# Holding attention's loads back to about 1.2 MB on their way, and issuing each input in two halves

## The chip, the cores and the metric

The kernel runs on one core of one Trainium2 chip. The metric is device microseconds of one execution, and the time given for a kernel is the median of several. One more execution is taken with the hardware profiler; all rows below come from that one. MB are 10^6 bytes, KB are 1024 bytes.

## The reference

All inputs are fp32. A retention (linear attention with a decay instead of a softmax) of 4 batches, 8 heads, 576 positions and 64 channels per head feeds two feed-forward layers over 2304 tokens, with a width of 512 and an inner width of 2048:

```python
scores = (1 / sqrt(64)) * q @ k.T
ret = scores * Dmat            # Dmat[i, j] = gamma_h ** (i - j) for i >= j, else 0
x = (ret @ v) of all heads, as [2304, 512]
h = x @ w_in;  g = max(h, 0) + alpha * min(h, 0);  x = g @ w_out      # "moe"
h = x @ w_in2; g = h / (1 + exp(-1.702 * h));      out = g @ w_out2   # "moe2"
```

## The kernel before

The order on every engine is written out by hand. Work that is not a step's own is put into a list of events by `at(time, ...)`, and `run_to(time)` carries out those that are due, so an event's time is a place in the order and no microsecond.

**Attention** goes over 16 pairs of heads, `PAIRS`, one after the other; I call the work of one pair a step, 0 to 15. In step i, TensorE computes the scores of pair i (`a_scores`, tile `sc`, four chunks of 128 positions), the outer products of keys and values (`a_outer`, tile `st`), then for the pair before it the products within chunks (`a_within`, tile `av`) and across chunks (`a_across`). All its matmuls go through one helper, `mm`, at L353. VectorE multiplies the scores by the decay (`a_evac`, L386) and sums the states; ScalarE scales keys and states (L317).

**Attention's loads** are `a_load(i)`: the 1728 columns of q, k and v of a pair go into a tile `ld` (L309), and its 512 columns of keys in another layout into a tile `kts` (L311). A column is 128 partitions of 4 bytes, so a pair has 0.885 MB and 0.262 MB. Loads 0 to 2 go out before step 0; the first is cut into three transfers, the next two into two. Loads 3 and 4 follow at the end of step 0, and load i+4 at the end of step i. There are five buffers for `ld`, so load i+4 waits for the step that last read its buffer, which is step i+1 at its beginning, as the rows of SP show.

**The queue of SP** issues all of these. Between them, by events, it issues the first weights of layer 1, `w_piece` (L129): rows 0 to 5 of `w1`, two pieces of 1024 columns (0.524 MB) each, into a tile `raw`. Six of the twelve pieces are issued before load 15. Behind load 15 stand the other six, the stores of the first output weights (`plain_store`, L212 and L213), the stores of `evict` (L249, L250), and then the stores of attention's output (`a_store`, L479). Later weights are issued by GpSimd's queue. SP issues in order: a transfer that waits holds up all behind it. The framework counts the landings of SP's transfers in eight counters in turn, so each transfer also waits, before it is issued, for the one eight places ahead of it to have landed.

**From a row of weights to its use**: ScalarE runs `w_sat`, `w_range` and `w_top` (L133, L137, L141) over a landed row, VectorE `w_low` (L148), and both split it into a high and a low part. ScalarE and VectorE too work in order.

**Layer 1** begins when attention ends, with products `h` (L515) and `acc` (L556); layer 1's last part and layer 2 go through `product` (L697) on sums of blocks.

Of the kernel before, what the change touches and what calls it, by code (L numbers as in the profile page):

```python
# [17 lines left out]
DM, DFF = 512, 2048  # L18
# [8 lines left out]
SYNC = mybir.DependencyInfo(mybir.DependencyClass.Sync, mybir.DependencyReason.DATA)  # L27
# [12 lines left out]
NG = 5  # L40
SUM = {1: 0, 2: 1, 4: 2, 5: 3}
RING = ("w6", "X1", "w15", "X2", "X4")
HOME = (0, 7, 2, 3, 4, 5, 6, 15)


@with_exitstack
def kernel(
# [11 lines left out]
    nc = tc.nc  # L59
# [36 lines left out]
    def slot(tag, shape, dtype=F32, name="t"):  # L96
        if tag[0] == "X":
            n = int(tag[1]) - 1
            return xp[n // 2].tile(shape, dtype, tag=f"x{n % 2}", name=name)
        return (wp if tag[0] == "w" else cvp).tile(shape, dtype, tag=tag, name=name)  # L100
# [21 lines left out]
    raws, cvs, wi, wo, x_t, fs, hs = {}, {}, {}, {}, {}, {}, {}  # L122

    def w_load(key, src, home):
        raws[key] = slot(home, [128, 2 * DM, 2], I32, "raw")

    def w_piece(key, src, c, eng):
        f = src[key[1]].rearrange("p (f t) -> p f t", t=2)
        eng.dma_start(out=raws[key][:, c * DM:c * DM + DM], in_=f[:, c * DM:c * DM + DM])  # L129

    def w_sat(key):
        f = raws[key][:, :, 1].bitcast(F32)
# [23 lines left out]
    def w_tile(m, n):  # L156
# [6 lines left out]
        if j not in wi:  # L163
            wi[j] = wp.tile([128, 2, 2, DM], F32R, tag=f"w{HOME[j]}", name="wi")
        return wi[j][:, a], f[:, 0:DM]
# [86 lines left out]
    def bring_wi(j):  # L252
        wi[j] = wp.tile([128, 2, 2, DM], F32R, tag=f"w{HOME[j]}", name="wi")
        nc.gpsimd.dma_start(out=wi[j].bitcast(F32), in_=kept[j // 2][0])
# [8 lines left out]
    def row(key, src, home, load, when, eng):  # L263
        at(load[0], w_load, key, src, home)
        for c, t in enumerate(load):
            at(t, w_piece, key, src, c, eng)
        for t, fn in zip(when, (w_sat, w_range, w_top, w_low)):
            at(t, fn, key)
# [27 lines left out]
    def tmp(what, i, shape):  # L296
        tags = TMP[what]
        return wp.tile(shape, F32, tag=f"w{tags[i % len(tags)]}", name=what)

    halves = (slice(0, 64), slice(64, 128))  # L300
    def kts(i):
        return kts_t[i // 4 % 2][:, i % 4]

    def a_load(i):
        b, p = PAIRS[i]
        t = tmp("ld", i, [128, 1728])
        cuts = {0: (0, 512, 1152, 1728), 1: (0, 1152, 1728), 2: (0, 1152, 1728)}.get(i, (0, 1728))
        for n, (c0, c1) in enumerate(zip(cuts, cuts[1:])):
            nc.sync.dma_start(out=t[:, c0:c1], in_=qkv[b, p, :, c0:c1])  # L309
            if n == (i == 0):  # L310
                nc.sync.dma_start(out=kts(i), in_=kn[b, p])  # L311
        q = [t[:, j:j + 128] for j in (0, 384, 512, 640)] + [t[:, 768:832]]
        k = [t[:, j:j + 128] for j in (128, 256, 832, 960)] + [t[:, 1088:1152]]
        ld[i] = q, k, t[:, 1152:1728].rearrange("p (n d) -> p n d", n=9), t[:, 384:832]
# [272 lines left out]
    def gblk(s, j):  # L587
        if j not in g2:
            n = f"w{HOME[j - 2]}" if j > 1 else ("raw0", "X3")[j]
            g2[j] = slot(n, [128, NG, RN], name="g2")  # L590
# [73 lines left out]
    def r_split(n, q, lo):  # L664
        if n not in ws:
            ws[n] = slot(RING[n % 4], [128, 2, 4, 256], F32R, "ws")
        c = slice(2 * q, min(2 * q + 2, 4 - n % 2))
# [6 lines left out]
    def s_load(r, n):  # L674
        i, h = divmod(n, 2)
        if r:
            home = RING[n % 5]
        elif n in (3, 4):
            home = ("w13", "w8")[n - 3]
            xt2.pop(8 - n)  # L680
        else:
            home = RING[(n - 2 * (n > 4)) % 3]
        t = ws["s", n] = slot(home, [128, 4, 2, 256], F32R, "ws2")
# [243 lines left out]
    with tc.manual_schedule():  # L927
        kts_t = [wp.tile([128, 4, 512], F32, tag=f"w{n}", name="kts") for n in (9, 15)]
        for t, a in ((fades_sb, fades), (vtab_sb, vtab)):
# [5 lines left out]
            out=mask_sb, in_=mask_sb, pattern=[[1, 128]], compare_op=ALU.is_ge, fill=0.0, base=0,  # L935
# [10 lines left out]
        for i in range(3):  # L946
            a_load(i)
# [4 lines left out]
        for i in range(n_a + 1):  # L952
# [34 lines left out]
            for n in (3, 4) if i == 0 else (i + 4,):  # L987
                if n < n_a:
                    a_load(n)
# [4 lines left out]
            out=rise_sb, in0=alpha_sb, scalar1=-1.0, scalar2=1.0, op0=ALU.mult, op1=ALU.add  # L994
# [47 lines left out]
        for r in range(R):  # L1042
            z = r * 2 * NU
            for j in range(NJ):
                u = z + 7 * j
                for t, what in (
# [3 lines left out]
                    if r == 0 and j in (5, 6) and what in ("g22", "g12"):  # L1050
                        t = 8.01
# [114 lines left out]
```

## Time and profile before

| | |
|---|---|
| median of 3 runs | 809.49 us (806.51, 809.49, 809.51) |
| profiled execution, its own time | 809.11 us |
| its span in the profile | 807.4 us |
| PE busy | 795.0 us (98%) |
| DVE, ACT busy | 642.6 us, 528.9 us |
| attention | from the start to about 73.8 us, where the first `h` begins |

The execution's own time is 1.7 us longer than the span, in which the first and the last instruction lie. PE is TensorE's matmuls and PEld its weight loads; both come from one stream of instructions. "issue" in the chain of waits is time in which the engine waited for nothing that the profile shows. The profile lists DMA queues by number: q1 carries the transfers that SP issues, q8 and q14 are of the kind "instruction". A row of DMA issues gives the size of one transfer and the median time from its issue to its landing.

### The profile page before, as it was taken

To read this page: it belongs to the slowest core of one execution; us is meant where nothing else is said; L and a number is where in the kernel's file an instruction comes from. 1 tells how busy PE (TensorE), PEld (TensorE's weight loads), DVE (VectorE), ACT (ScalarE), POOL (GpSimd) and SP (SyncE) were. 2 spreads that over 40 slices of the span, in tenths; PEclk is the share of its full clock that TensorE was granted. 3 is DMA by queue.
4 is the path that set the end of the run, shared out by engine and by line. 5 is a ranking of instruction groups with operands and counts; after the bars stand their busy time and mean duration, and the time that the engine had idled before them with its cause. 6 is when DMAs were issued, how large, how long until landed. Compare 5 with 4: busy or idle time off the path is not lost.

```text
span 807.4 us, 14644 instructions
## 1 busy us (share of the span) xinstructions
PE 795.0 (98%) x5260; PEld 739.9 (92%) x5260; DVE 642.6 (80%) x1195; ACT 528.9 (66%) x959; POOL 83.8 (10%) x104
## 2 busy tenths in 40 slices
PE   9898999999999999999999999999999999999998
PEld 7787888888887888899999999999999999999998
DVE  7776997888485586879999898799777899787775
ACT  6687969887455657456678667667566666566552
POOL 2321122100011111634300000000000000000000
PEclk9999999999999999999999999999999999999999
DMA  9996999865779987597889656996544986446881
GB/s 351 400 347 267 347 325 342 320 240 216 266 248 374 369 279 233 192 335 262 313 345 351 222 166 202 343 313 234 161 136 148 354 289 214 141 131 216 277 276 63
DMA packets 87791, 214.11 MB, mean 265 GB/s; under 512 B 7971, under 2 KB 43811, under 8 KB 79014
## 3 DMA queue, kind: packets, MB, share of 16 engines
q1 hardware_dynamic: 80784, 187.99, 65.5%
q0 software_dynamic: 6784, 25.17, 9.1%
q8 instruction: 41, 0.67, 0.3%
q14 instruction: 32, 0.26, 0.1%
q10 hardware_dynamic: 150, 0.02, 0.0%
HBM read 152.59 MB, written 60.56 MB: 264 GB/s over the span
## 4 chain that ended last, share of the span: by engine, by line
PE 89%; DMA 4%; DVE 3%; issue 1%; SPq 1%; ACT 1%; DVEq 0%; POOLq 0%; ACTq 0%
PE acc L697 32%; PE h L697 25%; PE acc L556 13%; PE h L515 13%; PE av L353 4%; PE sc L353 2%; PE st L353 2%; DMA raw<-in_w_dram 1%; DMA rg<-raw 1%; DMA ws<-sp 1%; DMA ld<-in_qkv_dram 1%; SPq L498 1%; DVE raw L198 1%; DMA x<-part 0%; DVE g L523 0%
## 5 line engine op out<-in xcount | busy, mean ns | idle before, releaser
L108 DVE TENSOR_TENSOR gsf<-g,gsf 128x384 fp32r<-128x384 f32 (+1 forms) x272 | 156.4, 586 | 52.8 <-ACT gsf L103 51.6
L103 ACT ACTIVATE gsf<-g 128x384 fp32r<-128x384 f32 (+1 forms) x272 | 146.0, 542 | 74.7 <-PE acc L697 32.5
L556 PE MATMUL acc<-gsf,wo 128*128 128x512 f32 x576 | 138.3, 389 | 1.1 <-ACT gsf L103 1.1
L515 PE MATMUL h<-x,wi 128*128 128x512 f32 x576 | 138.1, 389 | 0.0
L697 PE MATMUL acc<-gsf,ws 128*128 128x384 f32 x768 | 135.2, 334 | 0.0
L697 PEld LDWEIGHTS acc<-gsf,ws 128*128 128x128 f32 x768 | 133.3, 188 | 0.2 <-ACT x L103 0.2
L556 PEld LDWEIGHTS acc<-gsf,wo 128*128 128x128 f32 x576 | 107.9, 188 | 24.4 <-ACT gsf L103 1.5
L515 PEld LDWEIGHTS h<-x,wi 128*128 128x128 f32 x576 | 108.1, 188 | 22.4
L697 PE MATMUL acc<-x,ws 128*128 128x384 f32 x660 | 128.3, 334 | 0.0
L697 PEld LDWEIGHTS acc<-x,ws 128*128 128x128 f32 x660 | 115.6, 188 | 0.3 <-ACT tm L103 0.3
L697 PE MATMUL h<-x,ws 128*128 128x384 f32 x540 | 107.7, 334 | 0.0
L697 PE MATMUL h<-gsf,ws 128*128 128x384 f32 x576 | 102.0, 334 | 0.1
L697 PEld LDWEIGHTS h<-gsf,ws 128*128 128x128 f32 x576 | 100.0, 188 | 0.4 <-ACT x L103 0.4
L697 PEld LDWEIGHTS h<-x,ws 128*128 128x128 f32 x540 | 94.8, 188 | 0.0
L178 DVE TENSOR_TENSOR tm<-h,tm 128x384 f32<-128x384 f32 x97 | 53.6, 553 | 26.9 <-PE h L697 21.5
L178 DVE TENSOR_TENSOR g<-g 128x384 f32<-128x384 f32 x114 | 63.0, 552 | 0.7
L523 DVE SCALAR_TENSOR_TENSOR g<-g,rise_sb,h 128x512 f32<-128x512 f32 (+1 forms) x49 | 36.3, 742 | 32.6 <-ACT g L528 32.4
L103 ACT ACTIVATE tm<-acc 128x384 f32<-128x384 f32 x62 | 30.5, 493 | 47.8 <-PE acc L697 46.3
L528 ACT ACTIVATE g<-h 128x512 f32<-128x512 f32 (+1 forms) x49 | 29.0, 591 | 38.8 <-PE h L515 38.2
L178 DVE TENSOR_TENSOR raw<-raw 128x256 f32<-128x256 f32 x116 | 45.5, 433 | 1.0
L129 POOL DMA_DIRECT2D raw<-in_w_dram x44 | 23.2, 533 | 176.6 <-DVE raw L178 67.9
L148 DVE SCALAR_TENSOR_TENSOR raw<-raw 128x1024 int32<-128x1024 int32 x32 | 39.3, 1228 | 2.6 <-ACT raw L141 2.6
(104 smaller groups left out, 930.1 us busy)
## 6 DMA issues: line engine op xcount, KB each, us to landing
ws<-sm SPq DMA_DIRECT2D x32, 1024.0 KB, 7.0
ws<-sp SPq DMA_DIRECT2D x24, 1024.0 KB, 5.9
raw<-in_w_dram POOLq DMA_DIRECT2D x44, 512.0 KB, 7.9
sm<-raw SPq DMA_DIRECT2D x32, 512.0 KB, 4.3
pad<-rg SPq DMA_DIRECT2D x48, 256.0 KB, 2.7
ld<-in_qkv_dram SPq DMA_DIRECT2D x13, 864.0 KB, 7.4
raw<-in_w_dram SPq DMA_DIRECT2D x20, 512.0 KB, 8.0
r<-raw SPq DMA_DIRECT2D x16, 512.0 KB, 2.9
```

Source lines behind the costliest of these rows:

```text
L103: return nc.scalar.activation(out=out, in_=in_, func=ACTF.Copy)
L108: latest[0] = eng.tensor_tensor(out=out, in0=a, in1=b.bitcast(F32), op=ALU.subtract)
L129: eng.dma_start(out=raws[key][:, c * DM:c * DM + DM], in_=f[:, c * DM:c * DM + DM])
L148: latest[0] = nc.vector.scalar_tensor_tensor(out=g[:, 0:2 * DM], in0=t[:, :, 1], scalar=3, in1=t[:, :, 0], op0=ALU.logical_shift_left, op1 ...
L178: latest[0] = (eng or nc.vector).tensor_tensor(out=out, in0=x, in1=y, op=op)
L198: latest[0] = nc.vector.tensor_tensor(out=f.bitcast(F32R), in0=f, in1=hi, op=ALU.subtract)
L353: return nc.tensor.matmul(out=out, lhsT=lhsT, rhs=rhs, start=start, stop=stop, skip_group_check=True)
L515: nc.tensor.matmul(out=t, lhsT=w[:, cw, k * 128:k * 128 + 128], rhs=x[:, cx], start=(i == 0), stop=(i == 3 * NK - 1),)
L523: nc.vector.scalar_tensor_tensor(out=g[0], in0=g[1], scalar=rise_sb[:, m:m + 1], in1=h, op0=ALU.mult, op1=ALU.add)
L528: nc.scalar.activation(out=out, in_=in_, func=ACTF.Relu, scale=-1.0)
L556: nc.tensor.matmul(out=acc[0][d], lhsT=w[:, d // 2, cw, d % 2 * 128:d % 2 * 128 + 128], rhs=g[:, cx], start=(m == m0 and i == 0), stop=(m ...
L697: nc.tensor.matmul(out=out, lhsT=w(cw), rhs=x(cx), start=(start and n == 0), stop=True, skip_group_check=True,)
```

## The change

`paced` issues a transfer on SP's queue and makes it wait for the landing of an earlier one: going back over the transfers issued by `paced`, it adds up their columns, and the first at which the sum reaches 2300 columns (2300 x 512 bytes = 1.18 MB) is the one that must have landed. All loads of attention and the twelve pieces of `w1` on SP go through it; stores do not. Loads 3 to 15 go out as two halves of 864 columns, with the transfer of `kts` between them.

```diff
+FLYING = 2300
...
+    flying = []
+
+    def paced(out, in_, size):
+        ins = nc.sync.dma_start(out=out, in_=in_)
+        behind = 0
+        for other, n in reversed(flying):
+            behind += n
+            if behind >= FLYING:
+                tc.add_manual_dep(ins.ins, other.ins.name, SYNC, reason="transfers on their way")
+                break
+        flying.append((ins, size))
+
     def w_piece(key, src, c, eng):
         f = src[key[1]].rearrange("p (f t) -> p f t", t=2)
-        eng.dma_start(out=raws[key][:, c * DM:c * DM + DM], in_=f[:, c * DM:c * DM + DM])
+        out, in_ = raws[key][:, c * DM:c * DM + DM], f[:, c * DM:c * DM + DM]
+        if eng is nc.sync and key[0] == 1:
+            paced(out, in_, 1024)
+        else:
+            eng.dma_start(out=out, in_=in_)
...
     def a_load(i):
...
-        cuts = {0: (0, 512, 1152, 1728), 1: (0, 1152, 1728), 2: (0, 1152, 1728)}.get(i, (0, 1728))
+        cuts = {0: (0, 512, 1152, 1728), 1: (0, 1152, 1728), 2: (0, 1152, 1728)}.get(i, (0, 864, 1728))
         for n, (c0, c1) in enumerate(zip(cuts, cuts[1:])):
-            nc.sync.dma_start(out=t[:, c0:c1], in_=qkv[b, p, :, c0:c1])
+            paced(t[:, c0:c1], qkv[b, p, :, c0:c1], c1 - c0)
             if n == (i == 0):
-                nc.sync.dma_start(out=kts(i), in_=kn[b, p])
+                paced(kts(i), kn[b, p], 512)
```

On SP's queue, loads 5, 6 and the first piece of `w1` stood like this before (`DMAHW0` to `DMAHW7` are the eight counters of landings, each reached by every eighth transfer; `PE` and `Pool` stand for the readers of the buffer):

```order
L309 DMA ld_293<-in_qkv_dram 128x1728 [waits DMAHW1_49,PE_49,Pool_49]
L311 DMA kts_127<-in_kn_dram 128x512 [waits DMAHW2_49]
L309 DMA ld_366<-in_qkv_dram 128x1728 [waits DMAHW3_49,PE_49,Pool_49]
L311 DMA kts_127<-in_kn_dram 128x512 [waits DMAHW4_49]
L129 DMA raw_393<-in_w1_dram 128x1024 [waits DMAHW5_49]
```

With the change the same stretch, and load 7 behind it, stands like this:

```order
L131 DMA ld_295<-in_qkv_dram 128x864 [waits DMAHW6_49,PE_49,Pool_49]
L131 DMA kts_127<-in_kn_dram 128x512 [waits DMAHW7_49]
L131 DMA ld_295<-in_qkv_dram 128x864 [waits DMAHW0_49]
L131 DMA ld_369<-in_qkv_dram 128x864 [waits DMAHW1_49,PE_49,Pool_49]
L131 DMA kts_127<-in_kn_dram 128x512 [waits DMAHW3_49]
L131 DMA ld_369<-in_qkv_dram 128x864 [waits DMAHW4_49]
L131 DMA raw_397<-in_w1_dram 128x1024 [waits DMAHW5_49]
L131 DMA ld_439<-in_qkv_dram 128x864 [waits DMAHW2_49,DMAHW7_49,PE_49,Pool_49]
L131 DMA kts_127<-in_kn_dram 128x512 [waits DMAHW0_49]
L131 DMA ld_439<-in_qkv_dram 128x864 [waits DMAHW1_49]
```

A transfer's counter there is no longer that of the transfer eight places ahead but of one three to five places ahead: the first half of load 5 waits for the second half of load 3, and the second half of load 7 for the piece of `w1` in front of load 7.

On TensorE's queue, the scores of a step had one wait for their input before:

```order
L353 MATMUL sc<-ld 64x128 [waits DMAHW6_49]
L353 MATMUL sc<-ld 64x128 [waits DVE_49]
L353 MATMUL sc<-ld 64x128 x14
L353 MATMUL st<-ld,kts 64x64 [waits DMAHW7_49,PE_49,Activation_49]
L353 MATMUL st<-ld,kts 64x64 [waits Activation_49]
```

With the change, at step 3, they have a second one in the middle, at chunk 2, for the second half:

```order
L370 MATMUL sc<-ld 64x128 [waits DMAHW7_49]
L370 MATMUL sc<-ld 64x128 [waits DVE_49]
L370 MATMUL sc<-ld 64x128 x6
L370 MATMUL sc<-ld 64x128 [waits DMAHW1_49]
L370 MATMUL sc<-ld 64x128 x7
L370 MATMUL st<-ld,kts 64x64 [waits DMAHW0_49,PE_49,Activation_49]
L370 MATMUL st<-ld,kts 64x64 [waits Activation_49]
```

Nothing else is moved on TensorE's queue, and on the other engines only the numbers of the counters differ.

## Rows read from the trace of the kernel before

**Rows 1.** The page, part 1: busy time, share of the span, instructions of each engine

```profile
PE 795.0 (98%) x5260; PEld 739.9 (92%) x5260; DVE 642.6 (80%) x1195; ACT 528.9 (66%) x959; POOL 83.8 (10%) x104
```

**Rows 2.** The chain in order of time, within attention: start us, us, what

```profile
21.46 0.61 PE st L353 x16
...
24.98 0.62 PE st L353 x16
...
26.24 0.37 issue
...
32.25 0.27 issue
...
37.64 1.44 issue
...
49.76 0.51 issue
...
56.03 0.42 issue
...
61.33 2.38 issue
...
68.16 0.99 PE sc L353 x30
69.15 0.62 PE st L353 x16
```

**Rows 3.** Stretches: us, busy (instructions) by engine, granted clock, DMA share, GB/s

```profile
24.00:72.00 48.00, 42.60 (x978) 37.41 (x974) 34.11 (x76) 32.49 (x63) 12.61 (x11) 0.96 0.99 370
...
64.00:68.00 4.00, 4.00 (x61) 3.67 (x64) 2.97 (x8) 1.32 (x3) 0.00 (x0) 0.61 1.04 424
```

**Rows 4.** PE by line, 56.4 to 62.5 us: xcount, busy us, mean ns, idle before

```profile
L353 PE MATMUL sc<-ld 64*64 64x128 f32 x63 | 2.3, 272 | 0.0
L353 PE MATMUL av<-r,ld 128*64 128x128 f32 (+1 forms) x24 | 1.7, 255 | 0.0
L353 PE MATMUL av<-r 64*64 64x128 f32 (+1 forms) x21 | 1.3, 252 | 0.4 <-issue 0.4
L353 PE MATMUL st<-ld,kts 128*64 128x64 f32 x16 | 0.7, 228 | 0.0
L353 PE MATMUL st<-ld 64*64 64x64 f32 x4 | 0.3, 242 | 0.0
```

**Rows 5.** The page, part 3: a DMA queue's packets, MB, share of 16 engines

```profile
q8 instruction: 41, 0.67, 0.3%
```

**Rows 6.** DMA queues between 54.0 and 55.1 us

```profile
q8 instruction: 1, 0.02, 5.3%
```

**Rows 7.** DMA queues between 61.5 and 62.5 us

```profile
q8 instruction: 1, 0.02, 6.0%
```

**Rows 8.** DMA queues and issues between 24 and 56 us (issues: KB each, us to landing)

```profile
q1 hardware_dynamic: 3077, 12.11, 98.7%
...
ld<-in_qkv_dram SPq DMA_DIRECT2D x8, 864.0 KB, 7.0
```

**Rows 9.** DMA issues between 0.7 and 1.0 us: the kernel's first load

```profile
ld<-in_qkv_dram SPq DMA_DIRECT2D x1, 256.0 KB, 2.8
```

**Rows 10.** SP's queue in order of time, 53.2 to 63.5 us: start, us, issue

```profile
53.24 0.38 SPq L311 DMA_DIRECT2D kts<-in_kn_dram  x1
...
63.39 1.01 SPq L129 DMA_DIRECT2D raw<-in_w_dram  x1
```

**Rows 11.** DMA issues between 53.2 and 53.3 us: load 15's last

```profile
kts<-in_kn_dram SPq DMA_DIRECT2D x1, 256.0 KB, 7.2
```

**Rows 12.** DMA issues between 63.39 and 63.5 us: row 4's second piece

```profile
raw<-in_w_dram SPq DMA_DIRECT2D x1, 512.0 KB, 9.1
```

**Rows 13.** ACT in order of time, about 79.6 us: `w_sat` of row 4

```profile
79.64 1.15 ACT L133 ACTIVATE raw<-raw 128x1024 f32<-128x1024 f32 x1
```

## The prediction, made before the change was run

> **What bounds the kernel now.** I read the page's busy times first: PE is busy 795.0 us of a span of 807.4 [rows 1]. A change to loads can only win time in which PE idles or runs slowly, and only the stage of these loads, attention, is in question. So I went to the chain in order of time there [rows 2]. Look first for a step that nothing disturbs: from the outer products (st) of step 4 at 21.46 to those of step 5 at 24.98 it takes 3.52 us. Ten steps later, step 15 has its own at 69.15. That is 44.17 us for ten steps that at 3.52 would take 35.20: **8.97 us are lost** in them.
>
> Six idle pieces of PE stand there: 0.37 + 0.27 + 1.44 + 0.51 + 0.42 + 2.38 = 5.39 us [rows 2]. All are "issue": PE waited for no engine and no load. Right behind the longest the clock falls: in 64 to 68 the granted clock is 0.61 [rows 3], that is some 78% of 4 us at 1.2 GHz instead of 2.4, which costs half of 3.1 us, 1.6. The other 2.0 us lie in matmuls just behind an idle piece, which start without overlap, and in smaller hitches.
>
> What is PE waiting for? Count what it does from its restart at 56.45 (56.03 + 0.42) to the next stop at 61.33 [rows 2]: 63 + 24 + 21 + 16 + 4 = 128 matmuls [rows 4], each with its weight load, so 256 instructions. And the page has 41 packets on the instruction queue q8 [rows 5] for 2 x 5260 instructions of PE [rows 1]: 257 in each. One such packet moves at 54.0 to 55.1 [rows 6], shortly before the restart at 56.45; the next not before 61.5 [rows 7], shortly before the restart at 63.72. I conclude that **PE stops for its own next 256 instructions**, which come over the same 16 DMA engines as the loads. Nothing shows this directly; the count and the times do.
>
> How late are they? If a block is asked for when PE enters the one ahead of it, the time from one restart to the next is the fetch's round trip: 32.52 to 39.08 is 6.6 us, 50.27 to 56.45 is 6.2, 56.45 to 63.72 is 7.3. PE works through a block in 61.33 - 56.45 = 4.9 us. So fetches are late by 1.3 to 2.4 us. Meanwhile q1 takes 98.7% of the DMA engines, moving 12.11 MB in 32 us, or 0.378 MB/us, and a load takes 7.0 us to land [rows 8], though the kernel's first one, of 0.262 MB, took 2.8 [rows 9]. At 7.0 us there are 7.0 x 0.378 = 2.6 MB on their way.
>
> **The change, part by part.**
> *Less on its way.* When a transfer is let go, less than 1.18 MB is unlanded in front of it. In a stretch without weights the rest is 2240 columns (a half, a kts, a half), and with its own 864 that makes 1.59 MB instead of 2.6, so a landing after 1.59/0.378 = 4.2 us instead of 7.0. Of a fetch's 6.2 to 7.3 us, 2.2 lie behind its packet (61.5 to 63.72), and 4.0 to 5.1 in front of it. Scaled by 1.59/2.6 = 0.61 the latter become 2.4 to 3.1, the round trip 4.6 to 5.3, against 4.9 that PE needs. I take nearly all of the 8.97 us as won, -9.0, and leave 0.3 us for the one or two fetches at the upper end. Bounds of this remainder: 0, and 1.5 if four fetches are 0.4 late. With no idle piece of 2 us, the clock, which fell only behind that, should stay up.
>
> *The loads become the next limit.* Load 15's last transfer is issued at 53.24 [rows 10] and takes 7.2 us [rows 11]: landed at 60.45. Step 15's scores begin at 68.16, and without the 8.97 us would at 59.19. The DMA engines are full, so the landing hardly moves forward: 1.26 us. Do the new waits make holes? A lone transfer has a fixed part of 2.8 - 0.262/0.378 = 2.1 us. Behind a regular wait 2240 columns, 1.147 MB, are still to land, 3.0 us of work, which covers 2.1. Only where a half waits for a piece of w1 are 512 + 864 columns left, 0.705 MB or 1.86 us: a hole of up to 0.24 us, at six pieces, 1.4 us. I take 1.26 + 0.6 = +1.9; bounds 0 (slots free sooner, so loads issued sooner) and 2.7.
>
> *Thirteen more transfers* cost SP 0.38 us each [rows 10], beside its waits for buffers: nothing; without that cover 4.9 us spread over 50, still ahead of the steps. *The start*: loads 0 to 2 are cut as before and only go out a little later; I take 0, and as the upper bound one fixed part, 2.1.
>
> *ACT and DVE* are busy 32.5 and 34.1 us in 24 to 72 [rows 3]; squeezed into 41 us that is 79 and 83%: no bound. *Behind load 15* on SP stand six pieces of w1 and the stores. Row 4's second piece lands at 63.39 + 9.1 = 72.5 [rows 10, 12], and ACT takes it up at 79.64 [rows 13]: a gain of up to 7.1 us is covered even if this landing doesn't move. All later work hangs on PE and shifts as a whole.
>
> Sum: -9.0 + 1.9 + 0.3 = -6.8 us. On the profiled execution's own 809.1 us that is **802.3 us**. That execution stands 0.4 below the median shown, 809.49; the difference is inside the spread of its runs.
>
> **The rivals.**
> *A: the queue's depth isn't what delays a fetch.* If the engines serve the queues in turn, the number of loads that stand on q1 doesn't matter to a packet of q8, and all idle pieces stay: 809.1. For it: PE's blocks also cross a busy queue in steps 0 to 4 without a stop. Against it: a packet that follows five us after PE enters its block. The Trainium skill, "DMA: Bandwidth & Descriptors", section "Queues, rings and completion order", says that each DMA engine takes packets from its queues in turn; by that a fetch would wait for one packet of the loads, however many stand behind, and the sum would be 0. The Trainium skill, "Runtime: NRT & Kernel Launch", section "Instruction fetch mechanics", also has blocks of 256 instructions and calls crossing one mostly hidden; on the size the trace agrees (257), on the cost it does not (5.39 us idle). Chance 0.09.
> *B: the held queue runs dry now and then.* In SP's order 50 transfers up to load 15's last wait in this way. If each leaves the engines idle 0.1 us, load 15 lands at 65.45, and step 15 starts there instead of 68.16: 806.4. For it: at 98.7% the queue has no reserve [rows 8]. Against: 3.0 us of work against 2.1. Chance 0.20.
> *C, the other side: the same with 0.25 us a wait.* Load 15 lands at 72.95, 4.8 us after step 15 starts now: 813.9, slower. It decides from (68.16 - 60.45)/50 = 0.15 us, where the gain is gone. It needs the fixed part to exceed 3.0 us even with a short queue; the first load's 2.8 in all [rows 9] speaks against. Chance 0.05.
> *D: supply costs nothing,* SP's earlier issues make up for it: 800.1. Against: engines already full. Chance 0.11.
>
> **How the numbers follow.** Forecast 802.3, its own range 800.9 to 804.7: 0.55. A measurement of this kernel can tell about 0.5%, 4.05 us, from no change: faster is below 805.4, slower above 813.5. Faster: the forecast, D and a third of B, 0.73. Same: A and the rest of B, 0.22. Slower: C, 0.05. The range runs from 799.7, a little below D, to 807.0: 809.1 - 9.0 + 2.7 + 1.5 + 2.1 = 806.4 with every bound at its end, which takes in B; A and C lie outside.
>
> **What would show it.** In the changed kernel's chain, the "issue" pieces between 24 and 65 should shrink from 5.39 us to below 1, the clock stay near 1.0 in that stretch, loads land some 4 us after their issue (of which waiting on SP is no part), step 15's outer products come at about 62.3 instead of 69.15 and the first h at about 67. Idle PE that ends with a load (rivals B and C) would show as waits of sc for ld. It would be wrong if the issue pieces stay though loads land in 4 us (A), or if DMA's share in 24 to 56 falls well under 0.95 (B, C).

## The result, and the profile after

The changed kernel takes 815.9 us (median of 6 runs, 813.96 to 818.14) against 809.1 us for the kernel before on the same chip (6 runs, 806.51 to 809.85). The ratio is 1.0091, with a 95% interval of 1.0067 to 1.0115: **slower by 0.9%**, where 0.8% faster was forecast (6.8 of 809.1 us). The profiled execution took 813.96 us, 4.85 more than the profiled one before; its span is 812.3 us. All rows of "after" come from it.

I begin where the forecast began, with PE's busy time, and what it waits for until layer 1 is under way. First the page's part 1:

```profile
PE 795.7 (98%) x5260; PEld 740.2 (91%) x5260; DVE 643.2 (79%) x1195; ACT 528.1 (65%) x959; POOL 82.3 (10%) x104
```

PE does the same work as in [rows 1]. Its waits between 0 and 85 us (line, what it waited for, us in total, times, longest us):

```profile
PE sc L370 <- DMA ld<-in_qkv_dram: 6.7, 7, 2.0
PE st L370 <- ACT kts L334: 2.8, 1, 2.8
...
PE st L370 <- DMA ld<-in_qkv_dram: 0.9, 1, 0.9
```

No "issue" is left among them: the 5.39 us of idle pieces in [rows 2] are gone. In their place PE waits for loads and for ScalarE's keys. The stretches that answer to [rows 3], and the two that stand out:

```profile
48.00:52.00 4.00, 1.00 (x16) 0.60 (x16) 0.00 (x0) 0.62 (x1) 0.00 (x0) 0.72 0.94 344
52.00:56.00 4.00, 2.66 (x31) 2.55 (x32) 2.11 (x5) 3.28 (x6) 1.15 (x1) 0.50 0.90 289
...
64.00:68.00 4.00, 4.00 (x104) 3.66 (x102) 3.75 (x8) 3.95 (x8) 1.15 (x1) 1.00 0.90 303
...
24.00:72.00 48.00, 38.36 (x871) 32.91 (x869) 29.49 (x64) 29.52 (x57) 12.12 (x11) 0.93 0.90 301
```

PE is busy 38.36 us of these 48, where it was 42.60, and the core moves 301 GB/s, where it moved 370. The clock no longer falls in 64 to 68. It falls to 0.50 in 52 to 56, that is to 1.2 GHz, behind 4 us in which PE was busy 1.00. The DMA queues between 24 and 56 us, which answer to [rows 8]:

```profile
q1 hardware_dynamic: 3392, 9.54, 90.1%
...
ld<-in_qkv_dram SPq DMA_DIRECT2D x12, 432.0 KB, 4.7
raw<-in_w_dram SPq DMA_DIRECT2D x4, 512.0 KB, 5.5
kts<-in_kn_dram SPq DMA_DIRECT2D x6, 256.0 KB, 4.4
```

A transfer now lands in 4.7 us instead of 7.0, as the change intends. But in the same 32 us q1 moves **9.54 MB instead of 12.11**, 21% less. What SP waits for, 0 to 75 us, is the other side of it:

```profile
SPq L131 <- DMA ld<-in_qkv_dram: 21.4, 24, 2.6
SPq L131 <- DMA kts<-in_kn_dram: 16.0, 15, 2.5
SPq L131 <- DMA raw<-in_w_dram: 9.2, 6, 2.6
```

So all of attention's input comes later. In SP's queue in order of time, and among the DMA issues of 69.4 to 69.5 us, load 15's last half:

```profile
69.43 0.33 SPq L131 DMA_DIRECT2D ld<-in_qkv_dram  x1
```

```profile
ld<-in_qkv_dram SPq DMA_DIRECT2D x1, 432.0 KB, 4.2
```

It lands at 73.6 us; before, load 15 was there at 60.45 [rows 10, 11]. In the timeline of PE, step 15's outer products and the first product of layer 1:

```profile
75.00 0.69 PE L370 MATMUL st<-ld,kts 128*64 128x64 f32 x16
...
79.69 0.98 PE L532 MATMUL h<-x,wi 128*128 128x512 f32 x3
```

The former stood at 69.15 [rows 2]; the latter, in the trace of before, at 73.78. Attention ends 5.9 us later, and that is the main part of the loss. In the chain that ended last, attention no longer consists of PE's work but of transfers, each let go by the one in front:

```profile
39.83 5.96 DMA raw<-in_w_dram
45.79 0.02 issue
45.81 0.33 SPq L131
46.13 0.05 issue
46.19 5.17 DMA raw<-in_w_dram
51.35 0.02 issue
51.37 4.65 DMA ld<-in_qkv_dram
...
77.41 9.62 DMA raw<-in_w_dram
```

The last line is row 4's second piece, behind load 15 in SP's queue. It lands at 87.0, and layer 1 feels it (timelines of ACT and of PE; in brackets the idle time before and what ended it):

```profile
87.05 1.14 ACT L150 ACTIVATE raw<-raw 128x1024 f32<-128x1024 f32 x1 [0.91 <-DMA raw<-in_w_dram]
88.76 3.29 PE L573 MATMUL acc<-gsf,wo 128*128 128x512 f32 x12 [0.57 <-ACT gsf L104]
```

Matmul by matmul, PE is 5.9 us behind the kernel before at its first `h`, 7.4 at 104 us, and 5.2 at the end; of the 2.2 that come back, 1.1 are a wait for ScalarE that only the trace of before has.

One more thing meets the eye. Row 1's second piece, issued at 46.19, lands at 51.35, and ScalarE, which works in order, stands idle before it (timeline of ACT):

```profile
51.38 1.10 ACT L150 ACTIVATE raw<-raw 128x1024 f32<-128x1024 f32 x1 [6.00 <-DMA raw<-in_w_dram]
```

ScalarE's keys of the next step queue up behind that, and PE's 2.8 us for them is the longest wait in attention. Whether it is a cause is tested below.

### The profile page after: what moved, and what is told of

It reads as the page before. It is cut to its first block, busy times and chain, and to the rows that moved or that the text cites. A ratio compares the mean times of both kernels' runs of the same rounds, so it can differ in the third digit from the quotient of the medians.

```text
span 812.3 us, 14660 instructions
## 1 busy us (share of the span) xinstructions
PE 795.7 (98%) x5260; PEld 740.2 (91%) x5260; DVE 643.2 (79%) x1195; ACT 528.1 (65%) x959; POOL 82.3 (10%) x104
## 4 chain that ended last, share of the span: by engine, by line
PE 87%; DMA 10%; ACT 2%; SPq 1%; DVE 0%; issue 0%; DVEq 0%
PE acc L714 32%; PE h L714 25%; PE acc L573 15%; PE h L532 14%; DMA raw<-in_w_dram 5%; DMA ld<-in_qkv_dram 3%; DMA kts<-in_kn_dram 1%; SPq L131 0%; ACT raw L150 0%; ACT raw L158 0%; ACT gsf L104 0%; ACT g L545 0%; DVE raw L195 0%; DVE r L403 0%; ACT raw L154 0%
## 5 line engine op out<-in xcount | busy, mean ns | idle before, releaser
L150 ACT ACTIVATE raw<-raw 128x1024 f32<-128x1024 f32 x32 | 36.5, 1141 | 14.4 <-DMA raw<-in_w_dram 11.0
```

Source lines behind the costliest of these rows:

```text
L150: nc.scalar.activation(out=f, in_=f, func=IDENTITY_SAT240, scale=2.0 ** -9)
```

## The experiments

All times are medians; each ratio is to the kernel before in runs on the same chip. Two theories stood against each other at first: the waits starve the loads (theory 1), or the smaller transfers do (theory 2).

**1. Halves without waits.** The change with an endless window.

```diff
-FLYING = 2300
+FLYING = 1 << 30
```

> The halves stay, the new waits go (each transfer waits only for the landing of the one eight places ahead). Theory 1 (the waits leave too little on its way): q1 moves 0.36 to 0.38 MB/us in 24 to 56 us as before, issue pieces of PE of 3 to 6 us come back, PE waits for no load after step 4, time within 2 us of before. Theory 2 (the cut into halves is what costs, by smaller pieces and 13 more transfers): 0.31 to 0.34 MB/us, waits of sc for ld of 3 us and more, time 3 to 7 us over before.

807.4 us (10 runs), ratio 0.9976 [0.9955, 0.9998]. DMA, 24 to 56 us, and then PE's waits, 0 to 85:

```profile
q1 hardware_dynamic: 4348, 12.35, 100.0%
...
ld<-in_qkv_dram SPq DMA_DIRECT2D x16, 432.0 KB, 6.2
```

```profile
PE sc L370 <- issue: 3.8, 1, 3.8
PE st L370 <- issue: 1.3, 1, 1.3
...
PE av L370 <- issue: 0.9, 1, 0.9
```

Smaller transfers cost nothing, and with 12.35 MB moved the issue pieces are back, 6.0 us of them. Theory 2 falls.

**2. Waits without halves.**

```diff
-        cuts = {...}.get(i, (0, 864, 1728))
+        cuts = {...}.get(i, (0, 1728))
```

> The waits stay, the loads go out whole as before. Theory 1: up to 1.18 + 0.88 MB unlanded instead of 1.18 + 0.44, so a rate between the two kernels, 0.32 to 0.35 MB/us; PE still waits for loads, time 809 to 814. Theory 2: the rate is back at 0.36 or more and the issue pieces are smaller than before, time 803 to 808.

818.57 us (4 runs), ratio 1.0109 [1.006, 1.0159]. DMA, 24 to 56 us:

```profile
q1 hardware_dynamic: 2261, 8.88, 79.8%
...
ld<-in_qkv_dram SPq DMA_DIRECT2D x6, 864.0 KB, 6.7
...
kts<-in_kn_dram SPq DMA_DIRECT2D x6, 256.0 KB, 5.0
```

The waits alone are enough for the loss; whether the halves soften it isn't shown, since the intervals overlap. Theory 1 missed here: it had a rate between the two kernels and 809 to 814 us, and the rate is 8.88/32 = 0.278 MB/us, below that of the change (9.54). By its columns, a whole load may have 3968 columns unlanded with its own, 2.03 MB, as much as a half in experiment 3, which moves 11.47 MB. So the bytes that may be on the way don't decide alone; what else does, the size of the single transfers perhaps, was not tried.

**3. A wider window, 3400 columns (1.74 MB).**

```diff
-FLYING = 2300
+FLYING = 3400
```

> The change with 3400 columns (1.74 MB) instead of 2300 (1.18). Theory 1: the rate rises with the window, to 0.34 to 0.37 MB/us in 24 to 56; waits for loads fall under 4 us, some issue pieces come back (1 to 3 us); time 804 to 811. Theory 2: the rate stays at 0.30 to 0.32, and the time at 813 to 817.

807.48 us (10 runs), ratio 0.9991 [0.997, 1.0011]: no change. DMA, 24 to 56 us:

```profile
q1 hardware_dynamic: 3985, 11.47, 97.8%
...
ld<-in_qkv_dram SPq DMA_DIRECT2D x16, 432.0 KB, 5.4
```

PE's waits up to 85 us hold no issue, 0.2 us for loads, and 2.8 us for ScalarE's keys, behind ScalarE's 3.0 us for a piece of w1. The expected issue pieces of 1 to 3 us didn't come. So there is a depth at which the stops are gone and the rate is nearly kept; it wins back the loss, and no more. The clock falls all the same, behind the wait for the keys (stretches, as above):

```profile
48.00:52.00 4.00, 4.00 (x65) 3.67 (x65) 1.46 (x4) 2.50 (x5) 0.87 (x2) 0.60 0.98 375
```

**4. What are the stops?** The kernel before, with 16 more of the matmuls ahead of attention whose result isn't used.

```diff
-        a_fill(5)
+        a_fill(13)
```

> The kernel before with 13 instead of 5 products of the idle-filling loop at the start, each two matmul records with a weight load each: 16 matmul records more on TensorE's queue ahead of attention. If PE stops at the ends of blocks of 256 instructions, the stops move 16 matmuls towards earlier places of the program: the stop that was after 31 of 32 score matmuls in step 14 comes after about 15. If they belong to a place in the work (a buffer, a load), they stay where they were. The time is about 1 us more or the same.

A single run, 814.06 us; the profile has 5276 matmuls instead of 5260. The chain in order of time behind the stop in step 14, first of the kernel before (the stop itself is the 61.33 of [rows 2]) and then, with the stop, of this one:

```profile
63.72 0.32 PE sc L353
64.03 0.62 PE st L353 x16
```

```profile
63.38 2.47 issue
65.85 0.76 PE sc L353 x17
66.61 0.62 PE st L353 x16
```

Before, one matmul of the scores was left after the stop; here 17 are, 16 more. The stop stays at its place in TensorE's stream, counted from its start, while the program moves past it. No load, buffer or engine is tied to that place. The same holds of the other stops: counted over the matmul records of the traces, the kernel before stops behind matmul 475, 602, 729, 984, 1111 and 1239, this one behind 220, 475, 602, 857, 984, 1111, 1239 and 1366. These places lie in one row, 220, 348, 475 and so on to 1366, in steps of 127 or 128. What is left is the stream's own blocks, and that they are fetched: a packet of the instruction queue ends 1.3 us before the restart at 65.85 (DMA queues, 63.5 to 64.6 us).

```profile
q8 instruction: 1, 0.02, 5.5%
```

Read packet by packet, that is so in every trace here that has stops: 33 of over 0.08 us stand at these places, and each ends 1.2 to 1.6 us behind the end of a packet of q8.

The time was expected about 1 us higher or the same. It is above all 19 runs of the kernel before on that chip (805.36 to 810.97), and the stops add up to 9.3 us instead of 5.4. With one run, that stays open.

**5. Only the holes behind pieces of w1?** By its columns, a window of 2600 leaves the waits as they are where only loads stand, and lets go sooner around a piece. By theory 3, the forecast's own idea of where holes could come, the loss would vanish.

```diff
-FLYING = 2300
+FLYING = 2600
```

> The change with 2600 columns instead of 2300. In a stretch without pieces of w1 the awaited transfer stays the same (the sums are 2240 and 3104); only around a piece it moves, and a half no longer waits for the piece in front of it, but has 2400 columns still to land instead of 1376. Theory 1 (the supply goes down with the columns in flight everywhere): 0.30 to 0.32 MB/us in 24 to 56, time 813 to 817, hardly changed. Theory 3 (the hole is behind the pieces): 0.33 to 0.36 MB/us, waits for loads halved, time 807 to 811.

814.01 us (4 runs), ratio 1.0074 [1.0056, 1.0092]. DMA, 24 to 56 us:

```profile
q1 hardware_dynamic: 3479, 9.75, 91.7%
...
ld<-in_qkv_dram SPq DMA_DIRECT2D x13, 432.0 KB, 5.2
```

Theory 3 falls: it had 0.33 MB/us or more, 10.6 MB, and 9.75 is hardly more than 9.54. (One trace is one execution: experiment 9, whose waits on SP are those of the change, moves 8.84.) The supply is short behind every wait.

**6. One transfer at a time.**

```diff
-FLYING = 2300
+FLYING = 1
```

> Each paced transfer waits for the landing of the one just in front of it. This measures a transfer alone, at every size. With the fixed part of 2.1 us that the prediction took from the first load, 432 KB land 3.3 us after their issue, 512 KB 3.5, 256 KB 2.8. If the fixed part is larger in the midst of attention, as the 4.7 us of the change suggest, 432 KB take 3.8 us or more. Some 67 transfers one after the other: attention ends at 190 to 260 us, time 930 to 1000.

A single run, 929.15 us. DMA, 20 to 190 us:

```profile
q1 hardware_dynamic: 7909, 21.43, 43.4%
...
ld<-in_qkv_dram SPq DMA_DIRECT2D x26, 432.0 KB, 3.3
raw<-in_w_dram SPq DMA_DIRECT2D x9, 512.0 KB, 3.7
kts<-in_kn_dram SPq DMA_DIRECT2D x14, 256.0 KB, 2.6
```

A lone 256 KB take 2.6 us, close to the 2.8 of the first load [rows 9]. From 256 to 512 KB it is 1.1 us for 0.262 MB more, or 0.24 MB/us. By these rows a transfer alone moves at 0.24 MB/us, not at the 0.378 that I had put in, and its fixed part is 2.6 - 1.1 = 1.5 us, not 2.1. Attention ends at 185.6 us; it and the time are just under what I expected.

**7 and 8. The first output stores behind attention.** Behind load 15 SP has the stores of `plain_store(0)` and `evict(0)`. Here they are moved behind attention, with window 3400 (7) and on the kernel before, with nothing else changed (8).

```diff
-    at(14.0, plain_store, 0)
-    at(14.5, evict, 0)
+    at(half(0), plain_store, 0)
+    at(half(0), evict, 0)
```

> The window of 3400 columns, and the 2.1 MB of stores that evict and the first plain_store issue within steps 14 and 15 go out when layer 1 begins. If transfers around 55 to 65 us delay the fetch and the last pieces of w1, attention keeps its clock and its last steps run at 3.5 us: 801 to 806, faster than both. If the stores are hidden anyway: as e3_window_3400, 805 to 809.

> The kernel before with the same stores moved to the beginning of layer 1, nothing else. If the long stop in step 14 (2.4 us, and the clock behind it) is a fetch behind these transfers and those of the loads: the stop there shrinks below 1 us and 2 to 4 us are won, 804.5 to 806.5. If it comes from the loads alone: 808 to 810, no difference.

Seven: 805.02 us (9 runs), 0.9971 [0.9956, 0.9986]. Eight: 805.3 us (12 runs), 0.9966 [0.9951, 0.9982]. The stores are worth 0.3% by themselves; the window adds nothing to that. In the trace of eight the longest stop is 1.56 us instead of 2.38, where I had expected less than 1, and the mean granted clock 1.0; why the stores matter was not tried.

**9. ScalarE's wait for the piece.** The changed kernel, with row 1 converted later.

```diff
-        (1, "raw0", (5.5, 6.5), (8.75, 9.75, 10.75, 12.0), 12.25, 13.0),
+        (1, "raw0", (5.5, 6.5), (10.75, 11.25, 11.75, 12.0), 12.25, 13.0),
```

> The changed kernel, with the four events that convert row 1 of w1 set later in the order (8.75, 9.75, 10.75, 12.0 become 10.75, 11.25, 11.75, 12.0); nothing on SP's queue moves. In the changed kernel ScalarE, which works in order, waited 6.0 us at 51.4 for the row's second piece, and TensorE then 2.8 us for ScalarE's keys at 56.1, with the clock at 0.50 in 52 to 56. Theory 1 (the in-order wait of ScalarE for this held piece makes a good part of the loss): TensorE's wait for ScalarE at 53 to 56 goes and the clock stays up there, the first h comes 3 to 5 us earlier than 79.7, and the time is 811 to 813. Theory 2 (the loads' own lateness sets the end of attention, and the wait for the piece lies beside it): TensorE waits the same time in sum, now for the loads alone, the first h stays within 1 us of 79.7 and the time at 815 to 817. Load 15's last half lands at 73.6 in the changed kernel, 0.0 to 1 us before or after step 15's scores, which speaks for theory 2.

815.93 us (4 runs), ratio 1.0089 [1.0067, 1.0111]: the same as the change. PE's waits, 0 to 85 us:

```profile
PE sc L370 <- DMA ld<-in_qkv_dram: 11.0, 9, 3.2
...
PE st L370 <- DMA ld<-in_qkv_dram: 0.7, 1, 0.7
```

The 2.8 us for ScalarE's keys are gone, and the wait for loads has grown from 6.7 to 11.0. The longest wait in the trace after was no cause: with it out of the way, PE stands before the loads instead. Theory 2 of this expectation holds by the waits and the median; the first h stands at 81.9 us and not within 1 us of 79.7, in a profiled execution of 818.6, the slowest of the four.

**10 and 11. Combinations.** Experiment 7 with row 1 later (10); halves without waits and the stores behind attention (11).

> The kernel with a window of 3400 columns and the stores behind attention (805.0), with row 1's conversion set later as well. There ScalarE waited 3.1 us at 45.3 for the row's second piece and TensorE 2.5 us for ScalarE's keys; no other wait of over 0.3 us stood in attention. With supply no limit at this window: the 2.5 us go, the first h comes at 69 to 69.5 instead of 71.5, and the time is 802 to 803.5. If the loads are next at once: TensorE waits for ld instead, and the time stays at 804.5 to 805.5.

> Halves without any wait (807.4) and the stores behind attention. If the gain of the stores (0.34% alone, on the kernel before) and that of the halves (0.24%) add up: 803.5. If both take time from the same stops for TensorE's next instructions: 805 to 806, with issue pieces of 3 to 4 us in sum still there.

Ten: 805.19 us (6 runs), 0.9948 [0.993, 0.9966]. Eleven: 806.49 us (12 runs), 0.9971 [0.9954, 0.9988]. Neither is told apart from experiments 7 and 8. In ten I had expected 802 to 803.5. In its trace PE waits 3.1 us for loads, and 3.0 us of issue are back although the window is the same, so at 3400 the stops are rarer, not excluded. Eleven is neither the 803.5 of gains that add up nor within 805 to 806; its trace has 8.5 us of issue. (Both profiled executions, 808.58 and 810.3 us, are the slowest of their kernels.) Experiments 7, 8, 10 and 11 are 0.3 to 0.5% faster than the kernel before; 8 is so with two lines.

**12. The pieces on another queue.** The changed kernel, with the twelve pieces of w1 issued by GpSimd, without a wait and outside the window.

```diff
-        layer1(m, home, load, when, hi, lo, nc.sync)
+        layer1(m, home, load, when, hi, lo, nc.gpsimd)
```

> The changed kernel (halves, window 2300), with the twelve pieces of w1 issued by GpSimd's queue instead of SP's: they no longer wait, no longer count in the window, and no longer stand between loads on SP. The waits of the loads for one another stay as they are. Theory 1 (attention's end is set by supply, and supply by the bytes that may be on the way): a piece now comes on top of the 1.59 MB, so more moves; the loads alone keep their rate of about 0.31 MB/us (1.59 MB in 4.7 + 0.4 us), load 15's last half lands at 62 to 65 instead of 73.6, the first h comes at 71 to 74 instead of 79.7 (3.5 us a step need 0.33 MB/us, a little more than that), 24 to 56 moves 10.5 to 11.5 MB instead of 9.5, and the time is 807 to 810. Theory 2 (each wait between loads leaves the queue idle, whatever else moves): the waits are as many, pieces or not, so the bytes of 24 to 56 stay at 9.5 to 10 MB, and the time at 813 or more.

811.63 us (12 runs), ratio 1.0028 [1.0013, 1.0043]. DMA, 24 to 56 us (q0 carries GpSimd's transfers):

```profile
q1 hardware_dynamic: 3160, 8.45, 73.2%
q0 software_dynamic: 796, 2.89, 24.6%
...
ld<-in_qkv_dram SPq DMA_DIRECT2D x15, 432.0 KB, 5.8
raw<-in_w_dram POOLq DMA_DIRECT2D x5, 512.0 KB, 6.7
```

The two queues and the rest move 11.42 MB, inside the 10.5 to 11.5 of theory 1, under the same waits between loads. But my time was too good, and so was the first h, which stands at 79.0. The pieces share the engines with the loads, a load takes 5.8 us to land instead of 4.7, and a queue that may have only 1.59 MB on its way then moves less: 8.45 MB, and load 15's last half lands as late as in the changed kernel (issued at 66.91, 6.5 us).

## Why the prediction was wrong

**The mechanism of the gain was right.** Experiment 4 shows that the stops belong to places in TensorE's stream and end behind packets of q8. How deep the loads' queue is moves these packets: counted from PE's entry into the block ahead, a packet starts after 3.5 us in the kernel before (median of nine blocks) and 3.7 in experiment 1, both without a window, after 2.4 at 2.03 MB (experiment 3) and after 1.5 at 1.59 MB (after). That answers rival A: the depth does delay what PE waits for. The stops add up to 5.4 and 6.0 us in the first two and are gone in the last two, but for 0.1 us in experiment 3. At 2.03 MB they are not excluded: 0.8 us in experiment 7 and 3.0 in 10, against 8.5 in experiment 11 without a window. Not shown is when PE asks for a block, which the prediction assumed. The Trainium skill, "DMA: Bandwidth & Descriptors", section "Queues, rings and completion order", has the engines serve their queues in turn, by which the depth would not matter to a stop; here it did (packets after 3.5 us against 1.5).

The size of the gain, -9.0 us, no run shows. The fastest kernels here win some 3 us: with the stops gone or short, PE meets the loads and ScalarE's keys (2.8 us in experiments 3 and 7). Nor does the clock hang on the stops alone: it fell to 0.60 in experiment 3 behind a wait for keys, and stayed at 1.00 behind a stop of 2.9 us in experiment 11 (64 to 72 us).

**The step that failed is "The loads become the next limit", +1.9 us.** With -9.0 and +0.3 as forecast, the 5.9 us by which the first h came late make it +14.6. Three things were put in there.
- *The rate as a constant.* "A landing after 1.59/0.378 = 4.2 us" took 0.378 MB/us, the rate of a queue that nothing held, and divided the new depth by it. In a held queue it goes the other way: the window and the time to landing bound the rate. The landing measured 4.7 us, so at most 1.59/4.7 = 0.338 MB/us can go through; measured were 9.54/32 = 0.298. The same quotient bounds the others: a window of 3400 columns lets 3104 columns stand in front of a half, 2.03 MB with its own, so 2.03/5.4 = 0.376, measured 11.47/32 = 0.358; the loads of experiment 12 1.59/5.8 = 0.274, measured 8.45/32 = 0.264.
- *"3.0 us of work, which covers 2.1."* Both numbers take the full rate; by the rows of experiment 6 they are 4.8 (1.147 MB at 0.24 MB/us) and 1.5. By these, too, nothing would run dry. The test itself was wrong: it looked for engines that stand idle, and more than half of what is missing isn't idle time. Against experiment 1, q1's packets fill 90.1% of the engines' time instead of 100.0%, which is 10% fewer bytes, and each takes 0.136 us instead of 0.118, which is 13%, of 23% in all. The Trainium skill's page "DMA: Bandwidth & Descriptors", section "Anatomy of one DMA — SWDGE (gpsimd) path", puts a transfer on GpSimd's path at 2.0 us plus its bytes at 436 GB/s. SP's transfers are listed as another kind (hardware_dynamic); by analogy, as an estimate, a window of 1.59 MB taken for one such transfer gives 1.59/(2.0 + 3.65) = 0.28 MB/us, a little below the 0.298 measured.
- *Holes only behind pieces of w1, 1.4 us in sum.* Experiment 5 widened just those: 9.75 MB instead of 9.54. The shortage is everywhere.

Put in numbers, load 15 landed at 73.6 and not at 60.45 + 0.6: 13 us behind the kernel before over 50 transfers, 0.26 us each. That is **rival C** by its numbers, 0.25 us, load 15 at 72.95 and 813.9 us, which was given 0.05; by its mechanism it is about half of it. It had the engines idle 0.25 us at each wait, and between 24 and 56 us they are idle 9.9% of 32 us, which is 3.2 us over 22 transfers, 0.14 us each. The rest is slower packets. What spoke against it, that its fixed part would have to exceed 3.0 us, was the wrong test. A right one stood in the rows: PE's undisturbed 3.52 us a step need 1.147/3.52 = 0.326 MB/us for the loads alone, and the pieces of w1 on top, so any fall from 0.378 by more than a seventh had to show in the end of attention.

**Of the smaller steps:**
- The remainder of 0.3 us for late fetches can't be read, since PE came late everywhere. The 4.9 us that PE needs for a block are one block's; the block ahead of it took 5.8 (50.27 to 56.03), which is why that fetch was late by 0.4 us and not by 1.3.
- Thirteen more transfers cost nothing: experiment 1 has them and is 0.2% faster than before.
- ScalarE and VectorE are no bound: 29.5 us each in 24 to 72. ScalarE's order did show, as 6.0 us before a piece, which the prediction missed by looking at row 4 alone; experiment 9 says that it didn't set the time.
- "Behind load 15" failed, even without the gain: row 4's second piece lands at 87.0 (77.41 + 9.62 in the chain) instead of 72.5 [rows 10, 12], and ScalarE and PE wait behind it (0.9 and 0.6 us).
- The tests named were the right ones: waits of sc for ld, and a DMA share "well under 0.95" in 24 to 56, which is 0.90, both as told for B and C.

## What to carry to other kernels

A queue that is let out by landings moves at most its window divided by the time from issue to landing at that depth; take that time from a row with about as many bytes on the way, cut into transfers of the same size, never from the full rate. Compare the result with what the consumers need at the pace you hope for, and if the margin is small, a shorter queue gives back what it wins. And a long wait in a trace is a suspect, no more: move it away, and see whether the next one takes its place.

## What was not expected of the hardware

- The DMA share hides a short supply: 21% fewer bytes went with a share of 90.1% instead of 98.7%. A packet simply took longer. In experiment 1, 4348 packets filled 100.0% of 32 us on 16 engines, 0.118 us each; after the change 3392 of nearly the same size filled 90.1%, 0.136 us each.
- Two groups of stores moved on SP made the kernel before 0.34% faster (experiment 8), more than any window gave.
- Stops and supply can come out even in the median: experiment 1 (6.0 us of stops and 12.35 MB in its trace) takes 807.4 us, experiment 3 (none and 11.47 MB) 807.48. The traces are of executions of 809.36 and 806.43 us, so how they come out even can't be read from them.
